# A hand-ordered transformer block on one core: c's load moved to ScalarE's queue, the last output tile in two parts, a gate row made later, and the middle in another order

## The chip, the cores and the metric

One core of a Trainium2 chip runs the whole program. The metric is the device time of one execution in microseconds (us); where several executions were timed, their median.

## The reference

x is 2048 rows of 448 (bfloat16). A vector c makes six rows of 448 by one matrix product; they shift, scale and gate two halves:

```python
mod = silu(c) @ w_mod            # six rows: sa, ca, ga, sb, cb, gb
h = layernorm(x) * (1 + ca) + sa
# A: 16 heads of 28; softmax features of q and k, both signs (56 a head)
kv = phi_k^T v ; z = sum(phi_k) ; o = (phi_q kv) / (phi_q z + 1e-6)
x = x + ga * (o @ wo)
h = layernorm(x) * (1 + cb) + sb
# B: gated MLP with a 2048x2048 mixing over the rows
z = gelu(h @ w_in)               # 2048 x 1792, halves z1 and z2
g = w_sp @ layernorm(z2) + b_sp
x = x + gb * ((z1 * g) @ w_out)
```

## The kernel before

The 2048 rows are 16 tiles of 128. The work is cut into some 700 small steps, and one long string, `ORDER`, holds their names in the order in which they are recorded. Each engine runs its own instructions strictly in that order, and a wait of one instruction holds all that stands behind it on the same engine or queue; so moving a word in the string moves an instruction on its engine. In a word such as `wM:15@B0` the number is the tile and `B0` the bank of PSUM that the matmul writes; a letter after a slash names the engine (V VectorE, S ScalarE, G GpSimd) or, for `ld:` words, the queue that issues the load (Y SyncE, S ScalarE). A matmul step into a bank waits until the step that read the bank before is done.

The program has these stages:

- **Start.** `ld:` words load c, the tiles of x (`x0` and `x1` are one tile each), the weights of k (`wk`) and so on. `du:n` (line 729) issues n matmuls of 256 columns on a zero tile into a bank that nobody reads. `ct` (line 740) turns the row of c by four small matmuls, `ce` makes silu of it on ScalarE and VectorE, `csA` and `ccA` (line 764) are sums of c with columns of w_mod. `FTk`/`ETk` turn the weights of k (822, 826), `PFk`/`EPk` fold the feature map and the scale into them (849, 796, 800). `l1s`, `l1e`, `l1r`, `l1a` normalise tiles of x (856 to 867), and `X` turns two of them on TensorE (880). Then the first product with k, `kM:1` (line 890), can run.
- **Attention**, to about 55 us: q, k and v products (lines 890, 898, 945), exponentials on ScalarE, and the sum over the rows (`kA`, 921). `gr` and `ge` (956, 959) make the two gate rows ga and gb in 128 equal copies; `wos` and `wts` multiply wo and w_out by them.
- **Middle**, to about 138 us: numerators (`nM`, 973), the output projection into x (`wM`, 1005) and its eviction with a row sum (`wR`, 1012), layer norm 2, then the products with w_in: `zM` (1049) for z2, `yM` (1078) for z1, each followed by a gelu on ScalarE. z2 is normalised by `zR` (moments, 1025 to 1032, GpSimd or VectorE), `zW` (the power -0.5 on GpSimd, 1035) and `zN` (1072). `T2` and `T3` are transposing DMAs on SyncE's queue, `W` (1086) those of w_sp.
- **Mixing**, to the end: the 2048x2048 product with seven instead of eight block products: `tT` (1102) and `sS` (1109) make differences of operands, `P` (1124) and `gM` (1145) are the matmuls, `d` and `x` (1133, 1140) the sums. `oM` (1159) is the product with w_out for one tile, `oE` (1162) adds x, `oD` (1165) stores the tile.

```python
def du(n, slot):
    wps = bank(slot, "warm_ps")
    for _ in range(n):
        nc.tensor.matmul(wps[:, 0, 0:256], lhsT=zero[:, 0:P], rhs=zero[:, 0:256], start=True, stop=True)

def oM(t, f0, f1, slot=None):
    if f0 == 0:
        ps["o" + str(t)] = bank(slot, "o_ps")
    for n in range(f0, f1):
        nc.tensor.matmul(ps["o" + str(t)][:, 0, 0:D], lhsT=later["z1T"][:, FO[n], t * P:(t + 1) * P], rhs=wout_s[:, FO[n], :], start=(n == 0), stop=(n == FC - 1))
```

Of the kernel before, what the change touches and what calls it, by code (L numbers as in the profile page):

```python
# [481 lines left out]
ORDER = """tbl du:8@B1 m2b/V ld:wk/Y du:3@A2 m2a/V du:11@A1 ld:c/Y ct@B0 ld:x1/S l1s:1 ld:x0/S l1s:0 m1/G ld:phi/Y ce:1 m3 FTk:1@B1 ce:2 l1e:1,2/G ld:wsa/Y du:2@A0  # L482
l1e:0,1/G FTk:0@A0 ld:wca/Y ce:3 ce:4 bd/V ld:x2/Y ld:wq/Y l1r:0,1 l1a:0/V du:6@A2 X:0@B0 ETk:0/S csA@A2 ETk:1/V PFk:2@B1 l1r:1,2 esA l1a:1/G X:1@A0 XE:0/V
m4 du:2@A2 FSk@B0 ccA@A1 FCk/S PFk:0@B0 ecA XE:1/S EPk:0/V EPk:2/S l1s:3 du:1@A2 PFk:1@A1 EPk:1/S ld:wv/Y l1s:2 PFk:3@A0 l1e:2,4/V EPk:3/S du:2@B0 kM:1@B1
FTq:1@A2 ETq:1/V ld:x3/Y FTq:0@B0 ETq:0/V kM:0@A0 kF:1 FSq@A2 FCq/V kE:1 kS:1 PFq:1@B0 scb kF:0 kE:0 l1r:2,4 l1a:2/G l1a:3/G l1s:4 X:2@B1 SHv@A1 PFq:2@A2
SCv:1/G EPq:1/S XE:2/S l1s:6 PFq:0@B0 SCv:2/G X:3@A0 l1s:5 kM:2@B1 SCv:0/S XE:3/S l1s:7 ld:x4/Y l1s:9 EPq:0/S SCv:3/G l1e:4,8/G l1s:11 kS:0 vM:2@A1 vM:3@B0
EPq:2/S vC:2 ld:wmgb/Y kE:2 PFq:3@A0 EPq:3/S ld:wmga/Y l1s:8 kM:3@A2 kF:2 qM:1@A1 kR:1 ld:x5/S l1r:4,8 vM:0@B1 kR:0 kS:2 kE:3 kF:3 vM:1@A2 l1s:10 qE:1
l1a:4/G gr:1@A0 vC:0 l1s:13 l1a:5/G vC:1 ge:1 gr:0@B1 l1a:7/G kS:3 l1a:6/G vC:3 T1:4,6 kP:0/G T1:6,8 qF:1 kR:2 ge:0 qM:0@A2 qE:0 kP:1/G l1s:12 kM:5@B0
kM:4@B1 kF:4 kP:2/V vM:5@A1 kA:0@A0 kE:4 l1e:8,12/G l1r:8,12 kA:1@A0 kA:2@A0 ld:wo/Y vM:6@B1 l1a:8/G kF:5 kE:5 kR:3 kP:3/V l1s:14 l1s:15 kM:7@B0 l1a:9/G
qF:0 kS:5 vC:6 kM:6@A2 l1a:10/G kS:4 vC:5 l1a:11/G qM:2@A1 kF:6 kR:5 kF:7 kR:4 kE:6 kP:5/V ld:wcb/Y qF:2 T1:8,10 kP:4/V kS:6 kR:6 vM:7@B1 kE:7 T1:10,12  # L490
kA:3@A0 wos:0/G l1e:12,16/G vM:4@A2 l1r:12,16 vC:7 qE:2 l1a:15/G kM:9@B0 kF:9 l1a:12/V l1a:14/G kM:8@B1 l1a:13/V vM:9@A1 kE:9 kS:7 kR:7 kF:8 vC:4 kS:9
kE:8 kS:8 T1:12,14 kM:10@B0 kP:6/G kE:10 kP:7/G kR:8 kF:10 kA:4@A0 kA:5@A0 kM:11@B1 kE:11 T1:14,16 kS:10 vM:10@B0 kF:11 kS:11 kA:6@A0 vC:9 kA:7@A0 kM:12@B1
kP:8/G kR:10 kE:12 kR:9 kP:9/V kR:11 vC:10 kP:10/V kF:12 kS:12 kM:13@A1 kR:12 vM:8@A2 kM:15@B0 vC:8 kF:13 kP:11/G kM:14@B1 ld:wsb/Y kE:13 kS:13 kR:13 kE:14
W:0,6 kF:14 kE:15 kA:8@A0 kA:9@A0 kP:12/V kS:14 vM:11@A1 kF:15 kS:15 kA:10@A0 vM:14@B1 kR:14 vC:11 vM:15@B0 vC:14 vM:12@A2 vM:13@B1 vC:12 kA:11@A0 vC:13
kP:13/G kA:12@A0 kR:15 kP:14/V kP:15/V wos:2/V kA:13@A0 kA:14@A0 vC:15 kA:15@A0 KV:0/V KV:1/V KZ:0 ld:win0/S qM:3@A2 KZ:1 nM:0@A1 qE:3 ld:wout/S nM:1@A0
nX:0 nX:1 qF:3 nC:0 csB@B0 W:0,1 ld:win1/Y nC:1 nS:0 ccB@B1 nT:0 qM:4@A2 qE:4 nA:0/V nT:1 ecB nA:1/V wos:3/V qM:5@A1 nM:2@A0 qF:4 esB nX:2 nM:3@A2 nX:3
FB@B1 wos:1/V nC:2 qE:5 T2:0,1 nC:3 nS:1 FBc/S qF:5 nT:2 nA:2/G wM:0/S@B0 nT:3 SHw:3@B1 wR:0/S SCw:0,3/S T2:1,2 nM:5@A1 nX:5 nM:4@A0 nC:5 nX:4 nC:4 nA:3/V
wQ:0/S wM:1/S@B0 wR:1/S SHw:2@B1 SCw:2,1/S qM:6@A2 SCw:0,0/S SCw:3,1/G nS:2 nT:5 nT:4 T2:2,4 nM:6@A1 wQ:1/V qE:6 nX:6 nM:7@A0 nA:5/G nA:4/V nX:7 SCw:0,2/S
qF:6 nC:6 nC:7 nS:3 nT:7 wM:2/S@B0 wR:2/S wM:3/S@B1 wR:3/S qM:7@A2 wQ:2/S nT:6 wQ:3/S nA:6/V SCw:1,1/V SCw:1,0/V nM:9@A0 T2:4,6 qE:7 nM:8@A1 wM:5/S@B1
nX:8 nX:9 wM:4/V@B0 l2R:0,2/G l2r:0,2 l2a:0/G T3:0,1 l2a:1/V qF:7 nC:8 wR:5/S zM:0@A2 gt nA:7/G l2R:2,4/G nC:9 nS:4 nT:9 nT:8 zG:0 l2r:2,4 l2a:3/G T2:6,8  # L500
wR:4/V l2a:2/G nM:10@A0 T3:1,2 T3:2,4 wQ:5/S nX:10 nA:8/V SCw:3,0/G wM:6/V@B1 wR:6/V nM:11@A1 wQ:4/S nX:11 nA:9/V SCw:2,0/V l2R:4,6/G zM:1@A2 nC:11 nC:10
zG:1 l2r:4,6 nS:5 l2a:5/V wQ:6/S wM:7/V@B1 l2a:4/G yM:0,0@B0 zM:2@A2 yG:0,0 T2:8,10 nT:10 wR:7/V zQ:1/V T3:4,6 W:1,3 zM:3@A0 zG:2 wM:8/V@A2 wQ:7/S l2R:6,8/G
W:0,5 wM:9/V@B1 nT:11 nA:11/V nA:10/V zG:3 wR:8/V zQ:0/S nM:12@A0 nM:13@A2 l2r:6,8 l2a:6/G zM:4@A1 wR:9/V nX:13 nX:12 T2:10,12 zR:0,2/G zQ:3/S wQ:8/S W:1,7
yM:0,4@B0 zG:4 yM:0,1@B1 zQ:4/S nC:13 nM:15@A1 nC:12 zW:0,2 nX:15 yG:0,1 nS:6 nT:13 wQ:9/S nM:14@A2 nX:14 l2a:7/G nT:12 zN:0/V zM:5@A0 yG:0,4 T3:6,8 l2R:8,10/G
# [25 lines left out]
def fast_path(tc, A_x, A_wqkv, A_w_phi, A_wo, B_w_in, B_w_sp, B_b_sp, B_w_out, c, w_mod, out, flag):  # L530
# [120 lines left out]
    def load_mod(eng, o, sec):  # L651
# [24 lines left out]
        "bsp": lambda q: q.dma_start(out=bsp[:], in_=B_b_sp.partition_broadcast(P)),  # L676
    }

    def ld(nm, eng):
        LOADS[nm](eng)  # L680

    def consts():
        nc.gpsimd.memset(wk_raw[0:CB, :, D:D + 16], 0.0)
# [3 lines left out]
        nc.vector.memset(zero[:], 0.0)
# [579 lines left out]
```

## Time and profile before

| what | value |
|---|---|
| median of 3 runs | 250.34 us (249.0 to 250.72) |
| the profiled execution | 249.4 us |
| its span, first to last instruction on the core | 247.6 us |
| TensorE busy | 240.5 us, 97% of the span |
| VectorE, GpSimd, ScalarE busy | 182.5, 116.3, 104.8 us |
| the granted clock of TensorE, mean | 0.996 |

The span leaves out 1.8 us around the program. Busy time of TensorE counts a matmul until its last column has been written, and consecutive matmuls overlap, so a share of 97% says that it seldom stands still, and not that every matmul is useful: the dummy matmuls count too.

### The profile page before, as it was taken

The page shows a single profiled execution, that of the slowest core. Times are in us where ns is not written, and L with a number is a line of the kernel's source. Part 1 is how long each engine was busy: PE and PEld are TensorE (multiplying, and loading weights), DVE is VectorE, ACT ScalarE, POOL GpSimd, SP SyncE. Part 2 cuts the span into 40 slices and gives each one's busy share as a digit, 9 for nine tenths or more (in the row PEclk, how much of TensorE's full clock was granted, in tenths as well). Part 3 has the DMA queues.
Part 4 walks back from the last instruction along what each step waited for, and adds up shares of the span by engine and source line. Part 5 has one row for each costly group of instructions (what it writes and reads, how often), then busy time and mean ns, then how long its engine had stood idle before and what let it go on. Part 6 is the DMA issues. An engine that isn't in the chain of part 4 may idle for free.

```text
span 247.6 us, 4188 instructions
## 1 busy us (share of the span) xinstructions
PE 240.5 (97%) x1533; PEld 126.8 (51%) x1533; DVE 182.5 (74%) x369; ACT 104.8 (42%) x217; POOL 116.3 (47%) x175
## 2 busy tenths in 40 slices
...
GB/s 178 293 217 102 193 86 177 194 113 178 51 72 110 127 162 136 163 158 176 179 177 0 162 181 173 0 1 0 3 0 37 0 0 3 56 0 37 21 95 65
DMA packets 68207, 25.22 MB, mean 102 GB/s; under 512 B 58129, under 2 KB 67602, under 8 KB 68178
## 3 DMA queue, kind: packets, MB, share of 16 engines
...
q8 instruction: 14, 0.23, 0.4%
...
HBM read 8.87 MB, written 1.84 MB: 43 GB/s over the span
## 4 chain that ended last, share of the span: by engine, by line
PE 85%; POOL 6%; ACT 3%; DVE 2%; DMA 1%; issue 1%; POOLq 0%
PE g_ps L1124 29%; PE o_ps L1159 9%; PE z_ps L1049 7%; PE q_ps L945 6%; PE k_ps L890 5%; PE v_ps L898 5%; PE g_ps L1145 5%; PE z_ps L1078 4%; PE x_ps L1005 4%; PE kvacc L921 3%; PE warm_ps L729 3%; PE num L973 2%; POOL f_zv L1035 1%; DMA f_hT<-f_xpad 1%; DVE f_z2n L1072 1%
## 5 line engine op out<-in xcount | busy, mean ns | idle before, releaser
L1133 DVE TENSOR_TENSOR f_zb<-g_ps,f_zb 128x512 f32<-128x512 f32 (+1 forms) x31 | 20.5, 670 | 17.1 <-PE g_ps L1124 16.7
L1124 PEld LDWEIGHTS <-f_z2n 128*128 128x128 bf16 x192 | 18.8, 98 | 22.7 <-issue 0.3
L1140 POOL TENSOR_TENSOR f_z1T<-f_zb,f_z1T 128x512 bf16<-128x512 f32 (+1 forms) x11 | 12.0, 1102 | 33.6 <-DVE f_zb L1133 33.6
L1049 PE MATMUL z_ps<-f_ar,f_hT 112*128 112x448 bf16 (+1 forms) x128 | 26.6, 352 | 0.0
L1140 POOL TENSOR_TENSOR f_z1T<-f_Sx,f_z1T 128x512 bf16<-128x512 f32 x6 | 8.0, 1332 | 39.3 <-DVE f_Sx L1133 39.3
L1078 PE MATMUL z_ps<-f_hT,f_ar 112*128 112x512 bf16 x112 | 26.1, 379 | 0.0
L1159 PE MATMUL o_ps<-f_wout,f_z1T 128*128 128x448 bf16 x112 | 22.5, 352 | 0.0
L1124 PE MATMUL g_ps<-f_ar 128*128 128x512 bf16 x96 | 22.4, 379 | 0.0
L1081 ACT ACTIVATE f_z1T<-z_ps,f_zb 128x512 bf16<-128x512 f32 x28 | 18.2, 684 | 5.2 <-PE z_ps L1078 5.1
L950 ACT ACTIVATE f_Eq<-q_ps 112x1024 bf16<-112x1024 f32 x16 | 16.3, 1032 | 5.8 <-PE q_ps L945 5.8
L1049 PEld LDWEIGHTS <-f_hT 112*128 112x128 bf16 (+1 forms) x128 | 12.2, 97 | 11.6
L1078 PEld LDWEIGHTS <-f_ar 112*128 112x128 bf16 x112 | 11.0, 98 | 12.6
L893 ACT ACTIVATE f_E<-k_ps 128x448 bf16<-128x448 f32 x32 | 15.8, 555 | 3.8 <-PE k_ps L890 3.7
L989 DVE TENSOR_TENSOR f_ar<-num,f_w 128x896 bf16<-128x896 f32 x16 | 17.0, 1087 | 0.4
L904 DVE TENSOR_REDUCE f_ksum<-f_E 128x32 f32<-128x896 bf16 x16 | 16.9, 1064 | 0.5 <-ACT f_E L893 0.4
L1124 PE MATMUL g_ps<-f_Eq,f_z2n 128*128 128x512 bf16 x72 | 16.5, 379 | 0.0
L1159 PEld LDWEIGHTS <-f_z1T 128*128 128x128 bf16 x112 | 11.0, 98 | 10.7
L1053 ACT ACTIVATE f_zb<-z_ps 128x896 bf16<-128x896 f32 x16 | 14.6, 913 | 4.1 <-PE z_ps L1049 3.8
L1162 DVE TENSOR_TENSOR f_xpad<-o_ps,f_x 128x448 bf16<-128x448 f32 x16 | 9.9, 622 | 8.0 <-PE o_ps L1159 7.9
L945 PE MATMUL q_ps<-f_hT,f_Wq 113*128 113x512 bf16 (+1 forms) x64 | 15.0, 379 | 0.6 <-ACT f_Eq L950 0.6
L1124 PEld LDWEIGHTS <-f_ar 128*128 128x128 bf16 x96 | 9.4, 98 | 11.1 <-DVE f_ar L1102 0.2
L1005 PE MATMUL x_ps<-f_ar 112*128 112x448 bf16 x64 | 14.1, 352 | 0.3 <-DVE f_x L1012 0.3
...
## 6 DMA issues: line engine op xcount, KB each, us to landing
out_dram<-f_xpad SPq DMA_DIRECT2D x16, 112.0 KB, 1.7
...
```

Source lines behind the costliest of these rows:

```text
L904: nc.vector.tensor_reduce(out=ksum[:, i], in_=Er[i % NR][:].rearrange("p s (c f h) -> p (s c) h f", c=4, h=HP), axis=AX.X, op=ALU.add)
L945: nc.tensor.matmul(t[:, u, :], lhsT=Wq[0:KR[m], m, cc * CB:cc * CB + P], rhs=hT[0:KR[m], 4 * st:4 * st + 4, m, :], start=(m == 0), stop=(m ...
L950: nc.scalar.activation(out=Eq[st // 2][0:CB, 2 * c2:2 * c2 + 2, s, (st % 2) * 512:(st % 2 + 1) * 512], in_=ps["q" + str(n)][0:CB, :, :], f ...
L989: nc.vector.tensor_tensor(out=tr[i % 2][:], in0=numv(i)[:, :, :, 0:DH], in1=wr[i // 2 % 2][:, i % 2].unsqueeze(3).to_broadcast([P, 2, H, D ...
L1005: nc.tensor.matmul(t[:, 0, 0:D], lhsT=oT[0:CB, i % 4, cc, :], rhs=wo_s[0:CB, cc, :], start=(cc == 0 and not with_x), stop=(cc == KC - 1))
L1049: nc.tensor.matmul(t[:, hf, 0:D], lhsT=hT[0:KR[m], i, m, :], rhs=win_s[0:KR[m], m, FH + hf * D:FH + (hf + 1) * D], start=(m == 0), stop=(m ...
L1078: nc.tensor.matmul(t[:, 0, :], lhsT=win_s[0:CB, m, fc * P:(fc + 1) * P], rhs=hT[0:CB, 4 * st:4 * st + 4, m, :], start=(m == 0), stop=(m == ...
L1081: nc.scalar.activation(out=stage_b()["z1T"][:, fc, st * 512:(st + 1) * 512], in_=ps["y%d_%d" % (st, fc)][:, 0, :], func=ACT.Gelu_apprx_tan ...
L1124: nc.tensor.matmul(g, lhsT=sta[:, m, :], rhs=mov[:, m, :], start=(m == 0 and i in (1, 6, 7)), stop=(m == 7), skip_group_check=True)
L1133: nc.vector.tensor_tensor(out=o, in0=x, in1=y, op=ALU.add)
L1140: eng.tensor_tensor(out=z, in0=T[r][:, c0:c1], in1=z, op=ALU.mult)
L1159: nc.tensor.matmul(ps["o" + str(t)][:, 0, 0:D], lhsT=later["z1T"][:, FO[n], t * P:(t + 1) * P], rhs=wout_s[:, FO[n], :], start=(n == 0), s ...
```

## The change

Seven edits, all in the fast path:

- c is loaded first on ScalarE's queue, ahead of the first two tiles of x; it was second on SyncE's, behind the weights of k.
- VectorE's clearing of the zero tile comes first of all and covers the 256 columns that `du` reads, not 512.
- Dummy matmuls: before `du` 8, 3 and 11 stood ahead of `ct`; now 8 stand ahead and 9 behind it. Over the whole string there are 30 instead of 35. `csA` stands ahead of the first `X`, no longer behind it.
- The second gate row (`gr:1`, for w_out) was made in the attention stage, beside the first; now it is made among the first `wM`. Its load `wmgb` goes behind `wsb`. Other loads change place or queue: `x5` from ScalarE's queue to SyncE's, `wo` from SyncE's to ScalarE's, the halves of w_in swap queues, and the second half (`win1`) comes early.
- From there to `gM:1` the steps of the middle stand in another order, some on another engine or in another bank.
- `yM:2,1` comes behind `gM:0`, where it came ahead of `gM:1`.
- The last tile's product, sum and store are made in two parts, of 256 and 192 columns, the first stored from ScalarE's queue.

```diff
-ORDER = """tbl du:8@B1 m2b/V ld:wk/Y du:3@A2 m2a/V du:11@A1 ld:c/Y ct@B0 ld:x1/S l1s:1 ld:x0/S l1s:0 m1/G ld:phi/Y ce:1 m3 FTk:1@B1 ...
+ORDER = """tbl ld:c/S du:8@B1 m2b/V ld:wk/Y ct@B0 m2a/V ld:x1/S l1s:1 ld:x0/S l1s:0 m1/G ld:phi/Y ce:1 m3 du:9@A1 FTk:1@B1 ...
...
-oE:11 oD:11/Y x:1,2,8,0,256/G oM:12,0,7@B0 oE:12 oD:12/Y oM:13,0,7@B1 oE:13 oD:13/Y x:1,2,8,256,512/G oM:14,0,7@B0 oM:15,0,7@B1 oE:14 oD:14/Y oE:15 oD:15/Y
+oE:13 oD:13/Y x:1,2,8,256,512/G oM:14,0,7@B0 oP:15,0,256@B1 oE:14 oD:14/Y oP:15,256,448@B0 oF:15,0,256 oG:15,0,256/S oF:15,256,448 oG:15,256,448/Y
...
     def consts():
+        nc.vector.memset(zero[:, 0:256], 0.0)
...
-        nc.vector.memset(zero[:], 0.0)
...
+    def oP(t, a, b, slot):
+        o = ps["op" + str(a)] = bank(slot, "o_ps")
+        for n in range(FC):
+            nc.tensor.matmul(o[:, 0, 0:b - a], lhsT=later["z1T"][:, FO[n], t * P:(t + 1) * P], rhs=wout_s[:, FO[n], a:b], start=(n == 0), stop=(n == FC - 1))
+    def oF(t, a, b):
+        nc.vector.tensor_tensor(out=later["ot"][t % 4][:, a:b], in0=ps["op" + str(a)][:, 0, 0:b - a], in1=x_sb[:, t, a:b], op=ALU.add)
+    def oG(t, a, b, eng):
+        eng.dma_start(out=outv[t][:, a:b], in_=later["ot"][t % 4][:, a:b])
```

The first place is the start of ScalarE's program; L656 and L657 load the tiles 0 and 1 of x, L655 loads c.

```order
 L732 ACT_TABLE_LOAD
 L732 ACTIVATE f_warm<-f_warm 128x1
+L655 DMA f_c_row<-in_c_dram 1x448
 L657 DMA f_x<-in_A_x_dram 128x448
 L656 DMA f_x<-in_A_x_dram 128x448
```

c now stands ahead of both tiles of x.

The second place is VectorE in the middle of the program, before the change. L1012 is `wR`, the last of them `wR:10`, L1025 to L1032 are moments of z2, L1072 is `zN:2`.

```order
L1012 SCALAR_TENSOR_TENSOR f_x,f_s_88<-x_ps,f_x 128x448 x2
L1025 TENSOR_SCALAR f_zm<-f_zs_92 128x2
L1026 TENSOR_TENSOR f_sq<-f_zm 128x2
L1031 SCALAR_TENSOR_TENSOR f_zv<-f_zs_93,f_sq 128x2
L1032 TENSOR_SCALAR f_zv<-f_zv 128x2
L1072 TENSOR_SCALAR f_z2n<-f_zb,f_zm,f_zv 128x896
L1012 SCALAR_TENSOR_TENSOR f_x,f_s_88<-x_ps,f_x 128x448
```

And VectorE with the change, at the same stage; L1072 is `zN:1`, the first L1012 behind it `wR:10` and `wR:13`, the next `wR:12`.

```order
L1012 SCALAR_TENSOR_TENSOR f_x,f_s_88<-x_ps,f_x 128x448
L989 TENSOR_TENSOR f_ar<-num,f_w_106 128x896
L1072 TENSOR_SCALAR f_z2n<-f_zb,f_zm,f_zv 128x896
L995 TENSOR_TENSOR f_ar<-f_ar 128x4x112 x2
L1012 SCALAR_TENSOR_TENSOR f_x,f_s_88<-x_ps,f_x 128x448 x2
L1019 SCALAR_TENSOR_TENSOR f_ar,f_s_89<-f_x 128x448
L1012 SCALAR_TENSOR_TENSOR f_x,f_s_88<-x_ps,f_x 128x448
```

`wR:10` stood directly behind `zN:2` and the moments that lead to it; now it stands ahead of both, behind `zN:1`.

The third place is GpSimd at the end of the middle, before the change: L1025 to L1035 are the moments and the power of the last two tiles of z2, L1102 is `tT:1,2`.

```order
L1072 TENSOR_SCALAR f_z2n<-f_zb,f_zm,f_zv 128x896
L1102 TENSOR_TENSOR f_ar<-f_z2n 128x1024
L1035 TENSOR_TENSOR f_zv<-f_zv,f_mhalf 128x2
L1025 TENSOR_SCALAR f_zm<-f_zs_92 128x2
L1026 TENSOR_TENSOR f_sq<-f_zm 128x2
L1028 TENSOR_SCALAR f_zv<-f_zs_93 128x2
L1029 TENSOR_TENSOR f_zv<-f_zv,f_sq 128x2
L1032 TENSOR_SCALAR f_zv<-f_zv 128x2
```

And with the change (L1102 into f_xpad is `tT:4,0`, into f_ar `tT:2,2`):

```order
L1025 TENSOR_SCALAR f_zm<-f_zs_92 128x2
L1026 TENSOR_TENSOR f_sq<-f_zm 128x2
L1028 TENSOR_SCALAR f_zv<-f_zs_93 128x2
L1029 TENSOR_TENSOR f_zv<-f_zv,f_sq 128x2
L1032 TENSOR_SCALAR f_zv<-f_zv 128x2
L1035 TENSOR_TENSOR f_zv<-f_zv,f_mhalf 128x2
L1072 TENSOR_SCALAR f_z2n<-f_zb,f_zm,f_zv 128x896
L1102 TENSOR_TENSOR f_xpad<-f_z2n,f_ar 128x1024
L1102 TENSOR_TENSOR f_ar<-f_z2n,f_ar 128x1024
```

The subtraction `tT:1,2` stood ahead of the last tiles' moments and power; now these come first, behind them two other subtractions, and `tT:1,2` itself has gone to VectorE, behind `gM:1`.

90 lines of the change are left out of this document (46 added, 44 removed).

## The prediction

> **What bounds the kernel now.** I read the page's busy shares and its chain first, then the waits of TensorE, then the busy time by stretches.
>
> ```profile
> PE 240.5 (97%) x1533; PEld 126.8 (51%) x1533; DVE 182.5 (74%) x369; ACT 104.8 (42%) x217; POOL 116.3 (47%) x175
> PE 85%; POOL 6%; ACT 3%; DVE 2%; DMA 1%; issue 1%; POOLq 0%
> ```
>
> TensorE is busy for 240.5 of 247.6 us, and 85% of the chain that ended last is its own work. The next engine, VectorE, has a quarter of the span free. So an edit pays only where TensorE stands, or where matmuls disappear. The second view says where it stands: engine, what it waited for, total, count, longest.
>
> ```profile
> PE q_ps L945 <- ACT f_Eq L950: 0.6, 1, 0.6
> PE x_ps L1005 <- DVE f_x L1012: 0.3, 1, 0.3
> PE g_ps L1145 <- DVE f_z2n L1072: 0.2, 1, 0.2
> PE warm_ps L729 <- DVE f_Wk L800: 0.2, 1, 0.2
> ```
>
> Leaving out the first matmul's wait for the cleared tile, that is the whole list: four stalls, 1.3 us together. The third view gives the stretches between (start:end, length, then busy time and count of TensorE, weight loads, VectorE, ScalarE, GpSimd, then granted clock, DMA share, GB/s).
>
> ```profile
> 12.26:55.00 42.74, 42.74 (x358) 25.90 (x356) 39.39 (x81) 33.26 (x64) 29.34 (x33) 1.00 0.68 153
> 58.00:100.00 42.00, 41.98 (x319) 23.90 (x318) 38.64 (x96) 35.56 (x85) 27.10 (x57) 1.00 0.60 114
> 100.00:104.50 4.50, 4.25 (x23) 2.03 (x22) 2.40 (x10) 4.12 (x12) 4.20 (x6) 1.00 0.94 169
> 135.00:139.00 4.00, 3.76 (x19) 1.52 (x17) 3.82 (x6) 1.84 (x3) 1.12 (x2) 1.00 0.71 115
> 139.00:242.50 103.50, 103.50 (x494) 48.18 (x493) 70.81 (x100) 0.00 (x0) 29.89 (x19) 1.00 0.22 43
> ```
>
> From 12.26 us on TensorE has no hole except at 57, 103.7 and 137.9 us. Reordering the long stretches can therefore only keep what is there or spoil it; what can be won lies before 12.26 us, in the holes, and behind the last matmul.
>
> **The start.** These are TensorE's rows (start, duration, what), and the rows of the loads.
>
> ```profile
> 1.23 4.88 PE L729 MATMUL warm_ps<-f_zero 128*128 128x256 bf16 x22 [1.23 <-DVE f_zero L687]
> 6.04 0.53 PE L740 MATMUL ct_ps<-f_one,f_c_row 1*112 1x1 bf16 x4
> 6.50 0.69 PE L822 MATMUL tps<-f_ident,f_wk_raw 112*112 112x112 bf16 x8
> 7.88 0.82 PE L729 MATMUL warm_ps<-f_zero 128*128 128x256 bf16 x6
> 9.42 0.40 PE L880 MATMUL xt_ps<-f_ident,f_xpad 128*128 128x128 bf16 x4
> 12.10 1.04 PE L890 MATMUL k_ps<-f_Wk,f_hT 113*128 113x448 bf16 x4
> ...
> 0.90 0.27 DVE L687 MEMSET f_zero<- 128x256 uint32 x1
> 0.92 0.38 ACTq L657 DMA_DIRECT2D f_x<-in_A_x_dram  x1
> 4.78 0.63 DVE L856 BATCH_NORM_STATS2 f_st<-f_x 128x6 f32<-128x448 bf16 x1 [2.01 <-DMA f_x<-in_A_x_dram]
> 8.65 0.71 POOL L867 TENSOR_SCALAR f_xpad<-f_x,f_nm,f_rs 128x448 bf16<-128x448 bf16 x1
> 11.15 0.68 DVE L800 TENSOR_SCALAR f_Wk<-pf_ps,f_ca 113x448 bf16<-113x448 f32 x1
> ...
> f_x<-in_A_x_dram ACTq DMA_DIRECT2D x2, 112.0 KB, 4.0
> out_dram<-f_xpad SPq DMA_DIRECT2D x16, 112.0 KB, 1.7
> ```
>
> 22 dummies in 4.88 us are 0.22 each; six from 7.88 us take 0.82, about 0.11 each. So the array runs at half rate at first, and at full rate some 5.4 us after its first matmul, by about 6.6 us. The `ct` matmuls begin at 6.04, 0.07 ahead of the modelled end of the dummies: it is the number of dummies that places them. With the change the clearing is first and half as long, so dummies start at about 1.0; eight of them end at 1.0 + 8 x 0.22 = 2.75. Then `ct` waits for c. Its issue is at about 1.0 (the first place of ScalarE's queue), and it lands between 1.7 us (the store's figure) and 4.0 us (the figure of x on that very queue) later: 2.7 to 5.0, and I take the middle, 3.85. `ct` takes 0.5, nine dummies 9 x 0.22 = 2.0, and the turning of wk begins at about 6.3 instead of 6.50: a gain of 0.2. How much survives to 12.10 depends on two chains that it does not touch. GpSimd normalises tile 1 until 8.65 + 0.71 = 9.36, and the second `X` follows at 9.42; VectorE folds wk's scale at 11.15. The first goes with x, and both tiles of x are issued behind c, by one issue of 0.38 later. I take **0.1 gained**, between 0.4 gained (c early, both chains shorter since `csA` comes earlier) and 0.5 lost (x later by one issue, and a little of TensorE's own).
>
> The gate row `gr:1` and the five dummies:
>
> ```profile
> 23.32 1.68 PE L956 MATMUL gr_ps<-f_wmg,f_scb 112*128 112x448 bf16 x8
> ```
>
> Both gate rows are 1.68, less the overlap 4 x 0.19 = 0.76 for one. It leaves a stretch where TensorE is full and enters another that is full: **zero**. The dummies that go stood where TensorE waited for something else: zero too. ScalarE's queue gets seven issues instead of five, 0.4 each, but ScalarE is busy for only 42%, and for 33.26 of 42.74 us where most of them go; zero, and 0.8 lost if its evictions were what TensorE waits for there.
>
> **The middle.** First the chain at 100 us, then GpSimd, VectorE and TensorE at 130 to 139 us.
>
> ```profile
> 100.83 1.09 POOL f_z2n L1072
> 101.92 0.67 POOL f_zv L1035
> 102.61 0.51 DVE f_z2n L1072
> 103.13 0.55 DVE f_x L1012 x2
> 103.72 0.92 PE x_ps L1005 x4
> ...
> 130.11 2.12 POOL L1102 TENSOR_TENSOR f_ar<-f_z2n 128x1024 bf16<-128x1024 bf16 x1 [7.34 <-ACT f_ar L1017]
> 135.07 1.71 DVE L1072 TENSOR_SCALAR f_z2n<-f_zb,f_zm,f_zv 128x896 bf16<-128x896 bf16 x2 [6.42 <-POOL f_zv L1035]
> 134.87 2.75 PE L1145 MATMUL g_ps<-f_Eq,f_z2n 128*128 128x512 bf16 x12
> 137.87 1.04 PE L1145 MATMUL g_ps<-f_Eq,f_z2n 128*128 128x512 bf16 x4 [0.24 <-DVE f_z2n L1072]
> ```
>
> At 103.72 the product `wM:15` waits for bank B0, which `wR:10` frees, and `wR:10` stands behind `zN:2`, which waits for a power on GpSimd. With the change `wR:10` stands ahead, so the wait goes whole: `wR:10` can run about 2 us sooner. The stretch has 4.50 - 4.25 = 0.25 idle. A matmul of 448 columns is recorded as 0.35 but follows the one before by 0.19 when the array is full, so a stall costs its idle row and this hidden 0.16: 0.41. At 137.87 `gM:1` waits for the last normalised tiles of z2. VectorE waited 6.42 for their power, and this stood on GpSimd behind the subtraction of 2.12 at 130.11. That moves to VectorE behind `gM:1`, so the tiles come up to 2 us sooner; 0.24 + 0.16 = 0.40 goes. What is late next there is `zN:11`, now on GpSimd behind the last power: about 1.1 us by the row at 100.83, inside the 2.1 won. The stall of 0.6 at 57 us stays: `qM:4` still waits for `qF:3`. Sum 0.81; the new order of some 300 steps is bound to make a small wait somewhere, and I keep **0.7** (all of it and the small stalls, 1.2, to 0.9 lost, if GpSimd's or VectorE's other waits surface twice at the size of these).
>
> **The tail.** Last rows of TensorE, VectorE and the store, and VectorE's group of 256 columns.
>
> ```profile
> 239.76 3.38 PE L1159 MATMUL o_ps<-f_wout,f_z1T 128*128 128x448 bf16 x17
> 243.17 0.62 DVE L1162 TENSOR_TENSOR f_xpad<-o_ps,f_x 128x448 bf16<-128x448 f32 x1 [0.70 <-PE o_ps L1159]
> 243.83 0.43 SPq L1165 DMA_DIRECT2D out_dram<-f_xpad  x1
> L1133 DVE TENSOR_TENSOR f_zb<-g_ps,f_zb 128x256 f32<-128x256 f32 x2 | 0.8, 420 | 0.5 <-PE g_ps L1124 0.5
> 245.70:247.60 1.90, 0.00 (x0) 0.00 (x0) 0.00 (x0) 0.00 (x0) 0.00 (x0) 0.50 0.05 13
> ```
>
> The matmuls are the same columns in 14 instead of 7: (3.38 - 0.35) / 16 = 0.19 for 448, thus 0.11 for 256 and 0.08 for 192, the same sum. The second part's bank must wait for `oE:14`, about 0.1. The sum of 192 columns costs some 0.35 (0.42 for 256 and 0.62 for 448 are a line) instead of 0.62, and the other part lies beside the matmuls: 0.27 - 0.1, and the first store's share off the last one's data, some 0.1: **0.25 gained**, between 0 (the store's 1.7 us to landing does not shrink with its size) and 0.5. Nothing after 245.70 moves.
>
> **The sum.** The profiled execution took 249.4; 249.4 - (0.1 + 0.7 + 0.25) = 248.35. The median shown is 250.34, and this execution lay 0.94 below it, so the sum by the median would be 249.3. I take a point between, nearer to neither: **248.8 us**.
>
> **Rivals.**
> - *The array's warm-up slips.* Now 22 dummies keep it busy without a hole until 6 us; with the change it stands from 2.75 to c's landing, about 1.1 us. If the rise counts from an unbroken stretch, full rate comes 5.4 us after 3.85, at 9.3 instead of 6.6. TensorE is half filled with real work then, so of the 2.7 us a half is lost: 1.3, and 248.8 + 1.3 = 250.1. For it: the rows show one unbroken stretch before the rise. Against: the rows cannot tell a window of fixed places from a count. [...]
> - *The middle gives back what it wins.* `gr:1` with its eviction and load enters a stretch where ScalarE is busy for 35.56 of 42.00 and VectorE for 38.64; a new wait of the size of the old ones (0.4) at two or three places cancels the 0.7: 249.5 to 250.3.
> - *More than I count.* c lands at 2.7, the start gains 0.4, all small stalls go, 1.2, and the tail 0.5: 249.4 - 2.1 = 247.3.
> - *Slower than before.* The count starts anew at every hole, also the short ones: in the changed start every wait for a load or an eviction is one, until `kM:1` at about 12.1 us. Then full rate comes at 12.1 + 5.4 = 17.5, and the 10.9 us from 6.6 on run at half rate: 10.9 / 2 = 5.4 more, about 254. It decides when no stretch of 5.4 us without a hole lies ahead of 12.1. Against it: before, the fold stage has holes too (0.23 ahead of 11.88 in its wait row), and the rate held.
>
> **How the numbers follow.** The forecast 0.52, the slip 0.16, the middle giving back 0.17, more gained 0.11, slower 0.04. The forecast's own spread, from the bounds above, is 247.8 to 249.9. The range 247.4 to 250.6 takes in the slip and the giving back, and leaves out the end of more gained (half of its 0.11), the slower case (0.04) and a rest of the first three (0.08): 0.18. About 1% is what a measurement of this kernel can tell from no change; before, three runs lay 1.7 us apart. Faster by over 1% means under 247.84: the case of more gained and a tenth of the forecast, 0.16. Slower by over 1% means over 252.84: 0.04. Within 1%: 0.80.
>
> **What the changed profile would show.** Right: `ct` at 3.5 to 4.5 us and wk's turning at about 6.2; dummies of 0.11 each from 6.6 us on; no wait row for L1005 and none for L1145; the row for L945 still at 0.6; a last sum of 0.35 on VectorE. Wrong: dummies of 0.22 each behind 7 us (the slip); `ct` behind 5 us; the tile of x starting VectorE's statistics at 5.2 instead of 4.78; new wait rows of TensorE between 58 and 137 us, above all for L956, L1005 or L1078, that together pass 0.5; a last store whose landing takes over 2 us.

## The result, and the profile after

The changed kernel took 250.99 us (median of 20 executions, 250.37 to 251.41), the kernel before 249.57 (20, 248.8 to 250.76): a ratio of 1.0053, 95% interval 1.004 to 1.0065, some 1.3 us slower (1.42 by the medians). The prediction's sum had 1.05 us gained. The profiled execution has a span of 248.8 us (before 247.6) and took 250.72 in all (249.4). In the tables below, one execution each of middle_only (252.56) and tail_padded (892.01) counts as slow and is left out of the ratio.

The waits of TensorE after the change:

```profile
PE ct_ps L740 <- DMA f_c_row<-in_c_dram: 1.4, 1, 1.4
PE warm_ps L729 <- DVE f_warm L687: 1.0, 1, 1.0
PE q_ps L945 <- ACT f_Eq L950: 0.6, 1, 0.6
```

The waits at L1005 and L1145 are gone, the one at L945 stays, as forecast. New is the 1.4 for c. The start on TensorE in order of time (start, duration, what):

```profile
1.04 1.89 PE L729 MATMUL warm_ps<-f_zero 128*128 128x256 bf16 x8 [1.04 <-DVE f_warm L687]
4.29 0.53 PE L740 MATMUL ct_ps<-f_one,f_c_row 1*112 1x1 bf16 x4 [1.36 <-DMA f_c_row<-in_c_dram]
4.75 2.10 PE L729 MATMUL warm_ps<-f_zero 128*128 128x256 bf16 x9
6.65 0.95 PE L822 MATMUL tps<-f_ident,f_wk_raw 112*112 112x112 bf16 x8
8.79 1.49 PE L729 MATMUL warm_ps<-f_zero 128*128 128x256 bf16 x6
10.84 0.36 PE L849 MATMUL pf_ps<-f_BD,f_wTk 112*112 112x112 bf16 x4
11.23 0.40 PE L880 MATMUL xt_ps<-f_ident,f_xpad 128*128 128x128 bf16 x4
13.81 0.35 PE L890 MATMUL k_ps<-f_Wk,f_hT 113*128 113x448 bf16 x1
```

VectorE and GpSimd in the same stretch, then the issues of ScalarE's and of SyncE's queue:

```profile
7.47 0.63 DVE L856 BATCH_NORM_STATS2 f_st<-f_x 128x6 f32<-128x448 bf16 x1 [1.26 <-DMA f_x<-in_A_x_dram]
10.46 0.72 POOL L867 TENSOR_SCALAR f_xpad<-f_x,f_nm,f_rs 128x448 bf16<-128x448 bf16 x1
...
1.08 0.55 ACTq L655 DMA_DIRECT2D f_c_row<-in_c_dram  x1
2.09 0.45 ACTq L656 DMA_DIRECT2D f_x<-in_A_x_dram  x1
1.70 1.02 SPq L652 DMA_DIRECT2D f_wm<-in_w_mod_dram  x2
```

The first product with k begins at 13.81 instead of 12.10. Two things are late. The six dummies at 8.79 take 1.49 us, where six took 0.82 at 7.88 before: the array is still at half rate, and by the spacing of the matmuls that follow full rate comes at about 10.3, 3.6 us later than before (6.7). And the statistics of the second tile, which stood at 5.54 before, wait for their load until 7.47. (The column of the granted clock reads 1.00 in this first stretch at half rate too, in both kernels; it shows later falls only.) The two delays meet at the second `X`: TensorE's row ahead of it ends at 10.84 + 0.36 = 11.20, GpSimd has normalised x at 10.46 + 0.72 = 11.18, and `X` starts at 11.23. The rows of before that answer to the first, to the issue of tile 0 (L656) and to that of w_mod (L652):

```profile
5.54 0.59 DVE L856 BATCH_NORM_STATS2 f_st<-f_x 128x6 f32<-128x448 bf16 x1
1.34 0.44 ACTq L656 DMA_DIRECT2D f_x<-in_A_x_dram  x1
1.98 1.01 SPq L652 DMA_DIRECT2D f_wm<-in_w_mod_dram  x2
```

Tile 0 was issued 0.64 ahead of the two big loads of w_mod and is now issued 0.39 behind the first of them: c's issue went ahead of it on one queue, and c's place fell away ahead of w_mod on the other. The middle has no hole left at the two places:

```profile
100.00:104.50 4.50, 4.50 (x25) 2.24 (x23) 2.31 (x8) 4.44 (x11) 2.99 (x8) 1.00 1.27 163
135.00:139.00 4.00, 4.00 (x20) 1.59 (x18) 2.00 (x3) 2.28 (x4) 2.63 (x6) 1.00 0.00 0
```

The tail, VectorE and TensorE and the issue of the last store, then its transfer (queue, size, us from issue to landing):

```profile
242.69 1.62 PE L1170 MATMUL o_ps<-f_wout,f_z1T 128*128 128x256 bf16 x14
244.35 0.36 DVE L1173 TENSOR_TENSOR f_xpad<-o_ps,f_x 128x192 bf16<-128x192 f32 x1 [0.26 <-PE o_ps L1170]
244.73 0.33 SPq L1176 DMA_DIRECT2D out_dram<-f_xpad  x1
...
out_dram<-f_xpad SPq DMA_DIRECT2D x1, 48.0 KB, 2.6
```

And the last store of before:

```profile
out_dram<-f_xpad SPq DMA_DIRECT2D x1, 112.0 KB, 2.2
```

The last sum takes 0.36, as forecast, but the last store is less than half the size and lands 2.6 instead of 2.2 us after its issue.

So the 1.2 us of span split in three: start 13.81 - 12.10 = +1.71; from there to the issue of the last store 230.92 instead of 231.73, -0.81; from that issue to the end of the span 248.8 - 244.73 = 4.07 instead of 247.6 - 243.83 = 3.77, +0.30.

### The profile page after: what moved, and what is told of

Read it like the earlier page. It is cut to its first block, busy times and chain, and to the rows that moved or that the text cites. A ratio compares the mean times of both kernels' runs of the same rounds, so it can differ in the third digit from the quotient of the medians.

```text
span 248.8 us, 4202 instructions
## 1 busy us (share of the span) xinstructions
PE 241.2 (97%) x1535; PEld 127.8 (51%) x1535; DVE 180.0 (72%) x360; ACT 109.3 (44%) x225; POOL 125.4 (50%) x175
## 3 DMA queue, kind: packets, MB, share of 16 engines
HBM read 8.87 MB, written 1.84 MB: 43 GB/s over the span
## 4 chain that ended last, share of the span: by engine, by line
PE 95%; DMA 1%; ACT 1%; DVE 0%; issue 0%
PE g_ps L1124 29%; PE z_ps L1049 10%; PE z_ps L1078 10%; PE o_ps L1159 8%; PE q_ps L945 6%; PE g_ps L1145 6%; PE k_ps L890 5%; PE v_ps L898 5%; PE x_ps L1005 5%; PE kvacc L921 3%; PE num L973 2%; PE warm_ps L729 2%; DMA f_c_row<-in_c_dram 1%; PE tps L822 1%; ACT f_Eq L950 1%; PE pf_ps L849 1%
## 5 line engine op out<-in xcount | busy, mean ns | idle before, releaser
L1049 PE MATMUL z_ps<-f_ar,f_hT 112*128 112x448 bf16 (+1 forms) x128 | 26.0, 352 | 0.0
L1140 POOL TENSOR_TENSOR f_z1T<-f_Sx,f_z1T 128x512 bf16<-128x512 f32 x6 | 9.1, 1513 | 27.8 <-DVE f_Sx L1133 27.8
L1159 PE MATMUL o_ps<-f_wout,f_z1T 128*128 128x448 bf16 x105 | 21.2, 352 | 0.0
L945 PE MATMUL q_ps<-f_hT,f_Wq 113*128 113x512 bf16 (+1 forms) x64 | 15.0, 378 | 0.6 <-ACT f_Eq L950 0.6
L1159 PEld LDWEIGHTS <-f_z1T 128*128 128x128 bf16 x105 | 10.3, 98 | 10.0
L1162 DVE TENSOR_TENSOR f_xpad<-o_ps,f_x 128x448 bf16<-128x448 f32 x15 | 9.2, 622 | 7.3 <-PE o_ps L1159 7.2
L890 PE MATMUL k_ps<-f_Wk,f_hT 113*128 113x448 bf16 (+1 forms) x64 | 14.5, 352 | 0.0
```

What stands on the lines that cost most here:

```text
L890: nc.tensor.matmul(t[:, 0, 0:D], lhsT=hT[0:KR[m], i, m, :], rhs=Wk[0:KR[m], m, :], start=(m == 0), stop=(m == KC - 1))
L945: nc.tensor.matmul(t[:, u, :], lhsT=Wq[0:KR[m], m, cc * CB:cc * CB + P], rhs=hT[0:KR[m], 4 * st:4 * st + 4, m, :], start=(m == 0), stop=(m ...
L1049: nc.tensor.matmul(t[:, hf, 0:D], lhsT=hT[0:KR[m], i, m, :], rhs=win_s[0:KR[m], m, FH + hf * D:FH + (hf + 1) * D], start=(m == 0), stop=(m ...
L1140: eng.tensor_tensor(out=z, in0=T[r][:, c0:c1], in1=z, op=ALU.mult)
```

## The experiments

Each kernel was timed beside the kernel before on the same chip. "Outside" is the time of an execution less its span, the median over the timed ones; "k" is the start of the first product with k in the profiled one. There are 12 executions of each kernel, but 4 of x_first, 6 of hole_filled and hole_alone, 9 of start_undone and 10 of tail_padded.

| run | median us | before | ratio (95%) | outside us | k us |
|---|---|---|---|---|---|
| start_undone | 250.58 | 249.35 | 1.0049 (1.0029 to 1.007) | 2.68 | 12.71 |
| start_whole_undone | 250.21 | 249.54 | 1.0014 (0.9986 to 1.0041) | 2.61 | 12.25 |
| hole_filled | 252.24 | 249.35 | 1.0115 (1.0089 to 1.0142) | 1.87 | 13.89 |
| hole_alone | 251.41 | 249.35 | 1.0083 (1.0062 to 1.0104) | 1.83 | 14.39 |
| hole_clean | 250.40 | 249.45 | 1.0027 (1.0009 to 1.0045) | 1.86 | 13.81 |
| x_first | 253.02 | 249.35 | 1.0141 (1.0117 to 1.0166) | 1.92 | 15.44 |
| x0_on_sync | 249.53 | 249.58 | 1.0008 (0.9986 to 1.0031) | 1.83 | 13.55 |
| x0_on_sync_filled | 251.16 | 249.58 | 1.0048 (1.0018 to 1.0078) | 1.84 | 12.83 |
| csa_first | 249.26 | 249.54 | 0.9975 (0.9948 to 1.0001) | 1.82 | 12.31 |
| middle_only | 249.72 | 249.54 | 0.998 (0.995 to 1.001) | 1.83 | 12.51 |
| middle_filled | 250.88 | 249.45 | 1.0053 (1.0028 to 1.0077) | 1.97 | 12.84 |
| csa_and_middle | 249.53 | 249.58 | 0.9991 (0.9968 to 1.0014) | 1.84 | 12.40 |
| tail_only | 250.67 | 249.54 | 1.0048 (1.0017 to 1.0079) | 2.58 | 11.85 |
| after_old_tail | 250.16 | 249.45 | 1.0023 (1.0007 to 1.004) | 1.86 | 13.76 |
| tail_one_queue | 250.46 | 249.45 | 1.005 (1.0026 to 1.0075) | 2.50 | 12.17 |
| tail_padded | 250.93 | 249.58 | 1.0055 (1.0034 to 1.0076) | 2.59 | 12.25 |
| tail_fewer | 250.42 | 249.44 | 1.0037 (1.0014 to 1.0061) | 1.83 | 12.14 |
| dummies_halved | 249.43 | 249.44 | 0.9999 (0.9978 to 1.0021) | 1.86 | 12.21 |

### The start

Two theories stood against each other: W, the hole while c is awaited delays the full rate of the array; X, tile 0 of x lands late. Undoing the start first:

```diff
# start_undone: the changed kernel with
-tbl ld:c/S du:8@B1 m2b/V ld:wk/Y ct@B0 m2a/V ld:x1/S ... m3 du:9@A1 FTk:1@B1
+tbl du:8@B1 m2b/V ld:wk/Y du:3@A2 m2a/V du:11@A1 ld:c/Y ct@B0 ld:x1/S ... m3 FTk:1@B1
# start_whole_undone: also csA behind the first X and all else up to the first product with k as before
```

> The changed kernel with the start of before: c second on SyncE's queue, both tiles of x first on ScalarE's, 22 dummy matmuls ahead of ct and none behind it, the zero tile cleared as before. Middle and tail stay changed. Both theories put the loss into the start, so both expect the first product with k at 12.1 to 12.3 us again (13.81 in the changed kernel) and a time 0.3 to 0.9 us under before's, ratio 0.9965 to 0.999. A third view, that the middle or the tail loses, expects a ratio of 1.002 or more.

> The changed kernel with the whole start of before, also its order of csA and X (the run start_undone kept the changed order there). If the start alone is to blame, this equals the middle's gain with the tail's: ratio 0.995 to 0.998. If the tail costs 0.3 to 1.2 us, it stands that much above the run middle_only: 0.998 to 1.003. If the rest of the start's order did the harm in start_undone, its span is shorter by 0.5 us than there.

Both brought the first product with k back, to 12.71 and 12.25, but not the time: both carry the split tail, and in both 0.8 us more lay outside the span (below). By span, the medians are 247.8 and 247.55 against 247.5 and 247.7 of before, and 249.15 in the changed kernel: the start is worth 1.4 to 1.6 us of span. That start_undone did not come back whole in its profiled execution has its own cause, which the granted clock shows (window, then as in the prediction; the seventh figure is the clock):

```profile
4.50:11.20 6.70, 5.91 (x102) 5.01 (x101) 4.28 (x15) 1.66 (x4) 4.27 (x13) 1.00 1.11 266
11.30:14.60 3.30, 3.28 (x20) 2.20 (x20) 2.09 (x5) 1.91 (x4) 0.97 (x3) 0.50 1.13 312
14.70:246.70 232.00, 228.06 (x1396) 118.12 (x1404) 171.82 (x330) 104.14 (x216) 118.32 (x148) 1.00 0.48 93
```

The array was at full rate early, and fell back to half for one stretch of 3.3 to 3.5 us, behind a stretch in which it stood for 0.8 of 6.7 us. That was in no theory. Next, the hole and the late tile each by itself:

```diff
# hole_filled: the changed kernel with
-ld:c/S du:8@B1 ... m3 du:9@A1 FTk:1@B1
+ld:c/S du:16@B1 ... m3 du:2@A1 FTk:1@B1
# hole_alone: the kernel before with
-du:8@B1 m2b/V ld:wk/Y du:3@A2 m2a/V du:11@A1 ld:c/Y ct@B0 ... m3 FTk:1@B1
+du:8@B1 m2b/V ld:wk/Y m2a/V ld:c/Y ct@B0 ... m3 du:14@A1 FTk:1@B1
# hole_clean: the kernel before with
-du:8@B1 m2b/V ld:wk/Y du:3@A2 m2a/V du:11@A1 ld:c/Y
+du:8@B1 m2b/V ld:wk/Y m2a/V ld:c/Y
# x_first: the changed kernel with
-tbl ld:c/S du:8@B1 m2b/V ld:wk/Y ct@B0 m2a/V ld:x1/S l1s:1 ld:x0/S l1s:0
+tbl du:8@B1 m2b/V ld:wk/Y m2a/V ld:x1/S l1s:1 ld:x0/S ld:c/S ct@B0 l1s:0
```

> The changed kernel with 16 instead of 8 dummies ahead of ct and 2 instead of 9 behind it: TensorE has no hole of 1.4 us any more, all loads stay where the change put them. Theory W (the warm-up: the hole made full rate come at 10.3 instead of 6.7 us, and that delays the start) expects full rate by 5 to 8 us and the first product with k at 12.2 to 12.6, ratio to before 0.997 to 1.000. Theory X (tile 0 of x: issued behind c at 2.09 instead of 1.34 us, it comes behind the big loads of w_mod, VectorE takes its statistics at 7.47 instead of 5.4, and the second X follows 1.8 us late) expects full rate early as well, but the statistics still at about 7.4, the second X at about 11.2 and the first product with k at 13.6 to 13.9; ratio 1.004 to 1.007.

> The kernel before with only its dummies moved: 8 stay ahead of ct, 14 go behind it; every load stays as before. TensorE then stands from about 3 us to c's landing at about 5.2. Theory W expects full rate only at 8.6 to 12 us and the first product with k 1.0 to 1.8 us later, ratio 1.004 to 1.007. Theory X expects full rate late as well, but the second X at 9.4 to 9.9, the first product with k at 12.1 to 12.7 and a ratio of 1.000 to 1.002.

> The changed kernel with c third on ScalarE's queue, behind both tiles of x; dummies as in the change, so the hole of TensorE stays and grows a little. Theory X expects the statistics of tile 0 at 5.3 to 5.7, the second X at 9.4 to 9.9, the first product with k at 12.1 to 12.7 and a ratio to before of 0.997 to 1.000. Theory W expects full rate at 8 to 12 us and the first product with k at 13.4 to 13.9, ratio 1.003 to 1.007.

> The kernel before with 8 instead of 22 dummies ahead of ct and none behind it: TensorE stands from 3 us to c's landing at 5.2, loads as before, and no dummies stand in front of the turning of wk (in hole_alone they delayed it by 2 us). Theory W expects full rate only after 8 us, the turning of wk at 5.6, the first product with k at 12.5 to 13.5 and a ratio of 1.002 to 1.007. Theory X (only x's landing counts) expects the first product with k at 12.0 to 12.3 and 0.999 to 1.001.

hole_filled did what X expected. TensorE's rows and VectorE's second statistics:

```profile
4.61 0.53 PE L740 MATMUL ct_ps<-f_one,f_c_row 1*112 1x1 bf16 x4
6.99 0.82 PE L729 MATMUL warm_ps<-f_zero 128*128 128x256 bf16 x6
9.99 0.40 PE L880 MATMUL xt_ps<-f_ident,f_xpad 128*128 128x128 bf16 x4 [0.87 <-DVE f_xpad L867]
10.91 0.40 PE L880 MATMUL xt_ps<-f_ident,f_xpad 128*128 128x128 bf16 x4
13.89 1.65 PE L890 MATMUL k_ps<-f_Wk,f_hT 113*128 113x448 bf16 x4
...
7.15 0.63 DVE L856 BATCH_NORM_STATS2 f_st<-f_x 128x6 f32<-128x448 bf16 x1 [1.08 <-DMA f_x<-in_A_x_dram]
```

And its busy time and clock behind that:

```profile
12.90:16.20 3.30, 3.30 (x24) 2.23 (x22) 1.83 (x5) 1.95 (x5) 1.16 (x3) 0.50 1.11 310
```

No hole, full rate at 6.99 already (0.82 for six dummies), and the first product with k is no sooner: tile 0 still lands at 7.15, TensorE waits 0.87 for its normalised form, and the clock then falls to half from about 12.9 on. By the ratios it is some 1.5 us slower than the change itself. In the profiles 0.8 of that lies between the first product with k and the issue of the last store (231.70 instead of 230.92), where the clock is at half until about 16.3, and 0.6 behind that issue (4.71 instead of 4.07).

hole_clean did what W expected: loads as before (second statistics at 5.92), and still 13.81:

```profile
4.87 0.53 PE L740 MATMUL ct_ps<-f_one,f_c_row 1*112 1x1 bf16 x4 [1.75 <-DMA f_c_row<-in_c_dram]
7.68 1.49 PE L729 MATMUL warm_ps<-f_zero 128*128 128x256 bf16 x6
13.41 0.61 PE L729 MATMUL warm_ps<-f_zero 128*128 128x256 bf16 x2
13.81 1.51 PE L890 MATMUL k_ps<-f_Wk,f_hT 113*128 113x448 bf16 x4
```

Two dummies at 13.41 still take 0.61 (0.38 at full rate), and k's four matmuls 1.51 (1.04 before), so full rate comes only at about 15, some 8 us later than before: a longer slip than the 3.6 of the changed kernel. Over twelve executions it costs 0.95 us; the profiled one, at a span of 249.4, was the slowest of them (median 248.5). hole_alone, +2.06, overstates the hole: its 14 dummies behind `ct` also stood in front of the turning of wk, which began at 8.59 instead of 6.50. x_first was to separate the two and did not: with c third the hole grew (`ct` at 6.18), and the second statistics came at 6.80 all the same, with tile 0 issued at 1.55. In start_undone, where they came at 5.86, tile 0 was issued at 1.33 and, with c still on SyncE's queue, w_mod at 1.98 instead of 1.70. So X's cause may be as much w_mod moved up as tile 0 moved back; no run moves one of them alone.

```diff
# x0_on_sync: after_old_tail (below) with tile 0 first on SyncE's queue
-tbl ld:c/S du:8@B1 m2b/V ld:wk/Y ct@B0 ... ld:x1/S l1s:1 ld:x0/S l1s:0
+tbl ld:c/S du:8@B1 m2b/V ld:x0/Y ld:wk/Y ct@B0 ... ld:x1/S l1s:1 l1s:0
# x0_on_sync_filled: the same with du:16@B1 ahead of ct and du:1 behind it
# csa_first: the kernel before with
-du:6@A2 X:0@B0 ETk:0/S csA@A2 ETk:1/V
+du:6@A1 csA@A2 X:0@B0 ETk:0/S ETk:1/V
```

> The changed kernel with the last tile in one part, and tile 0 of x issued first on SyncE's queue, ahead of wk and of the big loads of w_mod; c stays first on ScalarE's queue, dummies as in the change, so TensorE's hole stays. To be held against the run after_old_tail (ratio 1.0023). Theory X (tile 0's landing) expects the second statistics at 5.7 to 6.2 instead of 7.42, the second X at 9.4 to 10.2 and the first product with k at 12.2 to 12.9, ratio 0.995 to 0.999. Theory W (the hole) expects full rate still at 8 to 11 us and the first product with k at 13.3 to 13.8, ratio 1.001 to 1.003.

> The same with 16 dummies ahead of ct and 1 behind it: neither hole nor late tile. Both theories expect full rate by 5 to 8 us and the first product with k at 11.8 to 12.5, ratio 0.994 to 0.998; if a window with too little work still falls to half rate between 8 and 16 us, 1.000 to 1.004, and the granted clock shows it.

> The kernel before with csA ahead of the first X (and the six dummies ahead of them in another bank), nothing else. If csA as filler between the first X and the second kept the array busy enough, X now waits about 0.6 us and the window of the clock around it can fall to half rate: in part of the executions 1 to 1.7 us more, ratio 1.001 to 1.004. Otherwise no change, 0.999 to 1.001.

x0_on_sync missed its setup: c now landed at once (`ct` at 2.86), so the hole went too, and the second statistics came at 6.71, now behind tile 1's at 5.94 (4.78 before). It is 0.6 us under after_old_tail. Its twelve executions fall into two groups: seven with a mean granted clock of 0.997 or more took 249.0 to 249.6, five with 0.992 or less took 250.1 to 251.5. The profiled one is of the second group:

```profile
5.50:12.10 6.60, 5.02 (x90) 4.23 (x91) 4.29 (x15) 1.54 (x4) 4.26 (x13) 1.00 1.12 252
12.30:15.50 3.20, 3.20 (x21) 2.13 (x21) 1.94 (x5) 1.82 (x4) 1.02 (x3) 0.50 1.12 312
```

In the 6.6 us ahead of the fall the array is busy for 5.02. The same stretch in the kernel before:

```profile
6.00:12.26 6.26, 5.97 (x107) 5.45 (x107) 4.34 (x15) 2.88 (x7) 4.22 (x12) 1.00 1.11 292
```

There it is busy for 5.97 of 6.26. But the two groups are not x0_on_sync's own. In the rounds timed beside these runs, 31 of 140 executions of the kernel before have a mean clock of 0.993 or less; their median is 250.54, that of the other 109 is 249.31. Of the changed kernel's 20 executions none is so low. The share in x0_on_sync (5 of 12) and in start_undone (3 of 9) is not clear of 31 of 140; in hole_filled (6 of 6) it is. That thin work brings the fall on is argued, not shown, and where an expectation here speaks of a window of the clock, the runs show only such a stretch at half rate, of 3.2 to 3.6 us. x0_on_sync_filled, with eight dummies fewer behind `ct`, ranged from 249.0 to 252.3. csa_first lost nothing by its median, so the order of csA and X is not the harm.

### The middle

```diff
# middle_only: start and tail of before, the middle of the change
# middle_filled: middle_only with du:9 for du:6 ahead of the first X and du:4 for du:1 ahead of PFk:1
# csa_and_middle: start_undone with the last tile in one part
```

> The start of before, whole (up to the first product with k, in its old order), the middle of the change, the last tile in one part as before. The theory that the reordered middle does win its two stalls expects no wait of TensorE at L1005 and L1145 and a ratio of 0.9960 to 0.9980 (0.5 to 1.0 us). The rival, that the middle gives back what it wins, expects 0.999 to 1.002 with new wait rows.

> The run middle_only with three more dummies ahead of the first X and three more ahead of the second fold product. If the windows in which the array does too little are what spreads middle_only's times (248.2 to 251.2), the spread shrinks and the median falls to 248.6 to 249.2, ratio 0.995 to 0.998. If the dummies stand in the way of real work, the first product with k comes 0.3 to 0.7 later and the ratio is 0.999 to 1.002.

> The start of before with csA ahead of the first X, the middle of the change, the last tile in one part. csa_first alone gave 0.9975 and middle_only 0.998; if both hold together 0.994 to 0.998, 0.7 us won by the middle. If windows of the clock fall to half rate as in start_undone, 0.999 to 1.003 with a wide spread.

The middle wins what was forecast in most of the traces: from the first product with k to the issue of the last store middle_only takes 243.48 - 12.51 = 230.97 and after_old_tail 244.70 - 13.76 = 230.94, against 231.73 before: 0.76 and 0.79. The stretch 100.00:104.50 of middle_only is full, too:

```profile
100.00:104.50 4.50, 4.50 (x25) 2.27 (x24) 1.90 (x7) 4.03 (x10) 3.28 (x8) 1.00 1.09 159
```

In two profiled executions it does not: start_whole_undone takes 243.76 - 12.25 = 231.51 and middle_filled 244.91 - 12.84 = 232.07. There TensorE waits once, at 82 to 83 us, for a transposing DMA. The rows of start_whole_undone and middle_filled, then of csa_first, whose middle is that of before and which waits longest (`yM` in all three; its line is L1033 in the first two):

```profile
PE z_ps L1033 <- DMA f_hT<-f_xpad: 0.6, 1, 0.6
PE z_ps L1033 <- DMA f_hT<-f_xpad: 1.0, 1, 1.0
PE z_ps L1078 <- DMA f_hT<-f_xpad: 1.3, 1, 1.3
```

So one execution can lose 0.6 to 1.3 us there with either middle; why the transfer is late in these three is open.

By the times the gain is not shown: 0.998 with an interval that holds 1, since middle_only scatters from 248.2 to 251.2 (it waited 0.9 us for the first X in the profiled execution). middle_filled was to narrow that and made it worse, 249.9 to 252.3. Of the parts put together in csa_and_middle nothing is clear of the kernel before: no version here beats it beyond its interval.

### The tail

```diff
# tail_only: the kernel before with
-oM:14,0,7@B0 oM:15,0,7@B1 oE:14 oD:14/Y oE:15 oD:15/Y
+oM:14,0,7@B0 oP:15,0,256@B1 oE:14 oD:14/Y oP:15,256,448@B0 oF:15,0,256 oG:15,0,256/S oF:15,256,448 oG:15,256,448/Y
# after_old_tail: the changed kernel with that line the other way round
# tail_one_queue: tail_only with oG:15,0,256/Y
# tail_padded: the kernel before with
+oM:14,0,7@B0 oM:15,0,7@B1 oE:14 oD:14/Y oP:15,256,448@B0 oE:15 oD:15/Y
# tail_fewer: tail_only with the first 22 dummies of 256 columns as 11 of 512
# dummies_halved: the kernel before with them as 44 of 128
```

> The kernel before with the last output tile in two parts and nothing else. The prediction's step expects 0.25 us gained, ratio 0.998 to 1.000. The rival from the traces of the changed kernels: the last store's data are ready only 0.1 us sooner, and its short rows land 2.6 to 3.3 us after issue instead of 2.2; and where the start was undone, the time outside the span was 0.9 us more than in any other kernel. It expects 0.3 to 1.2 us lost, ratio 1.001 to 1.005.

> The changed kernel with the last tile in one part, as before. If the split tail costs in the changed kernel what it costs alone (about 0.5 us of span; the 0.75 outside the span did not show in the changed kernel), this is 0.2 to 0.6 us faster than the changed kernel: ratio to before 1.003 to 1.005. If the split gains 0.25 as predicted, it is slower: 1.006 to 1.008.

> The kernel before with the last tile in two parts, but both stores from SyncE's queue. If the second queue makes the loss of tail_only (its end has to be waited for on another engine), the time falls to before's or 0.2 under it: ratio 0.999 to 1.001, and about 1.8 us lie outside the span again. If the short rows and the code fetched beside them make it, it stays at 1.002 to 1.005.

The split costs 1.1 us alone, and about 0.75 in the changed kernel (1.0053 against 1.0023, from different rounds). The second queue is not to blame: one queue gives the same loss (1.005 against 1.0048).

> The kernel before with seven more matmuls behind the last product (192 columns of the last tile once more, into a bank that nobody reads); the sum and the store of the last tile stay in one part. If the added instructions at the end (and the code loaded for them) make the loss of tail_only, 2.4 to 2.7 us lie outside the span and the ratio is 1.002 to 1.005. If the split sums and stores make it, 1.8 to 1.9 lie outside and the ratio is 0.999 to 1.001.

tail_padded leaves sum and store whole, adds seven matmuls behind the last product and loses 1.35: the added instructions make the loss, not the split stores. What changes with them is a load of the program's own code at the end. The view of transfers lists it by queue (packets, MB, share of 16 engines). In the kernel before, from 242.2 to 243.8, ahead of the last store's issue:

```profile
q8 instruction: 1, 0.02, 6.5%
```

6.5% of 16 engines over 1.6 us is one engine for 1.7 us. In tail_padded it falls into the window from 243.7 to 245.7 (4.0% of 16 engines over 2.0 us, one engine for 1.3 us), beside the last store, whose issue is at 243.98:

```profile
q8 instruction: 1, 0.02, 4.0%
...
out_dram<-f_xpad SPq DMA_DIRECT2D x1, 112.0 KB, 2.5
```
By the starts of the single transfers in the trace, this load begins 1.6 us ahead of the last store's issue in all eleven kernels with the tail of before, and the store's last packet is through 1.3 to 1.6 us after its issue. In the nine kernels with more matmuls at the end it begins between 0.2 ahead of the issue and 0.7 behind it, and the last packet is through 1.85 to 2.7 after it. That the packets wait on the engine that loads code is argued from these times; a run that moves the code load alone was not made.

The other part of the loss, 0.7 us outside the span, showed in all five kernels so far with 1560 matmuls on TensorE, and in none with fewer (up to 1559 in middle_filled, at 1.97; the changed kernel has 1555, since it drops five dummies and adds seven products). Two runs asked whether the number counts:

> The run tail_only with the first 22 dummies of 256 columns as 11 of 512: the same columns and the same time at the start, 1549 instead of 1560 matmuls. If the number of TensorE's instructions makes the time outside the span, it falls from 2.6 to 1.8 or 1.9 and the ratio from 1.0048 to 0.999 to 1.002. If the tail makes it, both stay.

> The kernel before with the first 22 dummies of 256 columns as 44 of 128: the same columns, 1575 instead of 1553 matmuls, the tail as before. If the number of instructions counts, 2.5 to 2.7 us lie outside the span and the ratio is 1.003 to 1.006. If the tail counts, 1.8 and 0.999 to 1.001.

tail_fewer came back to 1.83 outside the span, as the number would have it, though its span is 0.35 longer than tail_only's, so its time fell by less. dummies_halved has 1575 and stays at 1.86: the number alone is not the cause. What it is (where the end of the code falls, for one) stays open.

## Why the prediction was wrong

- **What bounds the kernel**: right. TensorE's holes and its early rate decided; none of the other engines became the bound.
- **The start, forecast +0.1 gained, measured 1.71 lost.** This step failed, twice. First, it priced tile 0's delay by one issue, 0.38; the statistics came 1.93 later. It counted the issue that c adds on ScalarE's queue and left out the one that it takes away on SyncE's, by which w_mod is issued ahead of tile 0; that this makes the delay is argued from the issue times. hole_filled shows that the late tile alone holds the second `X` at 10.91 (9.42 before) and, with the clock at half from 12.9 on, the first product with k at 13.9. Second, the sum took full rate from 6.6 us for granted and made the slip a rival at 0.16. The slip came (full rate 3.6 us later, where the rival had 2.7), and hole_clean shows that a slip alone can hold the product at 13.8, though in its slowest execution and with a slip of some 8 us; its median lost 0.95. In the profiled execution of the changed kernel both reach the second `X` almost together (11.20 and 11.18), so undoing one alone would have won little up to there: in hole_filled that `X` came 0.32 sooner. Which of the two decides in the other executions is not separated: x_first and x0_on_sync each moved both. c itself landed at 4.29, inside the bounds of 2.7 to 5.0.
- **`gr:1`, the dummies, the extra issues, forecast zero.** The path between start and tail is shorter by the middle's gain alone, so nothing contradicts the zeros for `gr:1` and the issues. For the dummies the reason, that they "stood where TensorE waited for something else", was not enough: in hole_clean 14 of them go, the loads stay, and full rate comes some 8 us later. In the profiled executions of start_undone, hole_filled and x0_on_sync the clock also fell to half for one stretch (0.50 in the rows above), and in csa_and_middle's its mean is 0.992; since 31 of 140 executions of the kernel before have a mean as low (0.993 or less), what dummies do to that is open.
- **The middle, forecast 0.7, measured 0.76 to 0.81 in three profiles.** Right, by its own reasons: both waits are gone, L945's stays, and `zN:11` was not late. The times do not show it.
- **The tail, forecast 0.25 gained, measured 0.30 lost behind the store's issue in the profile, 0.75 by the times.** Up to that issue the step was right. From the first matmul of the last tile to the last issue it took 244.73 - 242.69 = 2.04; before, with the tile's seven matmuls the last of the 17 from 239.76, it was 243.83 - 241.65 = 2.18. So 0.14 was gained, where the sum had 0.27 - 0.1. The last sum took 0.36 for 0.35 predicted, the matmuls start 0.11 and 0.08 apart as predicted, and the second part waited 0.11 for `oE:14`. (The row's 1.62 for 14 matmuls is 1.33 and this wait, and runs to the recorded end of the last one, 0.16 more.) What failed is the term of 0.1 for the store and "Nothing after 245.70 moves": the smaller store landed 0.4 later after its issue, and the code load moved, from 1.6 us ahead of the last store's issue (242.23) to 0.13 ahead (244.60).
- **The rivals.** The slip, 250.1, was the nearest; with the middle's gain in it and the tail's in place of its loss it is short by 0.9. That it is so near is in part luck: it prices a slip of 2.7 us and no late tile. The mechanism of the slower rival, that the count starts anew at every hole, does not hold: full rate came at 10.3 in spite of a small hole of 0.06 at 8.0 us. A late stretch at half rate did occur, but as one stretch of 3.2 to 3.6 us in the profiles of three runs, and not in the changed kernel's.
- **The spread and the base.** The lower end of the forecast's spread, 247.8, is its sum of best bounds; the upper end, 249.9, is not the sum of the worst. That sum, 0.5 and 0.9 lost and nothing gained by the tail, gives 251.25. The base was lucky, too: the three executions shown had a median of 250.34, the twenty have 249.57, and the same sum from there gives 248.5, further from the result.

On the clock the runs show this much: the falls last between 3.2 and 3.6 us (start_undone, hole_filled, x0_on_sync), full rate came 3.6 us later in the changed kernel and some 8 in hole_clean, and executions of one kernel differ in their mean granted clock (0.985 to 1.000 in x0_on_sync). What sets these lengths and what brings a fall on is not shown: in x0_on_sync the clock fell with the array busy for 5.02 of the 6.6 us ahead.
